# A linear-attention and MoE kernel: one queue for batch 0, a new order for its first stages, joined loads and stores

## The chip, the core and the metric

The kernel runs on one core of a Trainium2 chip. The metric is device time in microseconds (us) of one execution; where several executions are given, their median. The core has five instruction streams: PE (TensorE, matmuls; PEld is its weight loads), DVE (VectorE), ACT (ScalarE), POOL (GpSimd) and SP (SyncE, which here only issues DMAs). DMAs are issued from SP and from POOL, and run on 16 DMA engines. POOL's DMAs convert float32 to bfloat16 on their way.

## The reference

```
q, k, v: (8, 8, 576, 64) float32          # batch, heads, sequence, head_dim
w_in: (512, 2048), w_out: (2048, 512), beta: (2048,)

phi(x) = where(x > 0, x, exp(x) - 1) + 1
kv  = einsum('bhsd,bhse->bhde', phi(k), v)
z   = sum(phi(k), over s)
x   = einsum('bhsd,bhde->bhse', phi(q), kv) / (einsum('bhsd,bhd->bhs', phi(q), z) + 1e-6)
x   = x with heads side by side: (4608 tokens, 512)
h   = x @ w_in
out = (h * sigmoid(beta * h)) @ w_out      # (4608, 512) float32
```

## The kernel before

**Tiling.** The sequence of a batch is cut as 576 = 64 groups (g) x 9 (j). A load puts 64 groups of four heads on one half of the 128 partitions and those of the other four heads on the other half, so that each partition row is 9 x 64 numbers in one piece. The tokens of one j are 64 rows. Tokens of two j make a token tile of 128 (t = 0 to 3); the ninth j makes a tile of 64 (t = 4). Four tiles of a batch (512 tokens) are one block of the two large products; the 64 left over of all eight batches make a ninth block of 512 (`xT_tail`).

**A batch's attention.** `phi_part` (exp on ACT), `phi_relu` and `phi_min` (DVE) make phi(k) and phi(q). `kv_both` sums phi(k)'s products with v over the groups, with a column of ones for the denominators; a mask keeps the blocks that belong to one head. phi(q) is transposed, by `q_trans` on PE (a PSUM tile, then a copy) or by `q_trans_dma` (two DMA transposes on SP). `numer` makes numerators and denominators of one token tile, divides, and leaves it in `xs`; it has one PSUM buffer. `xs` is transposed into `xT` by `x_trans` (PE and a copy) or by `x_trans_dma` (SP).

**A block's products.** The H phase (`h_phase`) has 16 steps `ff` of four matmuls 128x512; each ends in a `silu` on ACT, which writes `g`. The Y phase (`y_phase`) has four token tiles of 16 matmuls; `y_out` copies each from PSUM to one of three `y_sb` buffers on DVE and stores it with two DMAs of 64 rows from SP (L309 to L312). H, Y and warm-up matmuls share four PSUM buffers (`mmps`); all transposes and `kv_both` share two (`miscps`).

**Order.** It is written out by hand: each engine runs its instructions in the order of the text. `at(side, n, ...)` places the next batches' attention between the steps of the phases. In the steady loop (from L495) batch b+1's `kv_both`, `numer` and x transposes stand in block b's H phase, batch b+2's phi, q transposes and loads in its Y phase. Batches 3 to 7 use DMA transposes for q and x, batches 0 to 2 PE transposes.

**The start (L90 to L124, L341 to L442).** Batch 0's k and q come half by POOL's casting DMAs, half by SP in float32 into `stage`; its v by POOL. `w_in` follows on POOL in four loads, then batch 1's k and q. `w_out` comes by SP in float32, the first part held back until the third `w_in` load has landed (`add_manual_dep`); half of it lies in `g_sb[1]`, which block 1's silu will overwrite, half in `stage`. It is scaled by 1/beta on its way to bfloat16: `w_out_scale`, parts 0 and 1 on DVE, 2 and 3 on POOL. `idle` issues warm-up matmuls on data that nobody needs. Block 0's first four H steps run in two column halves, beside batch 0's last token tiles. Block 0's Y phase goes over the parts i of `w_out`: 0, 1 and 2 for all four tiles, then batch 1's q transposes, kv and numerators with part 3 between them, then all four `y_out`.

The store's rows, which the change touches (L304):

```
    def rows(b, j):
        return out[b * S : (b + 1) * S, :].rearrange("(g j) m -> j g m", j=J)[j]
```

Of the kernel before, what the change touches and what calls it, by code (L numbers as in the profile page):

```python
# [16 lines left out]
def kernel(  # L17
# [51 lines left out]
    k0f = stage[:, 0:1152].rearrange("p (h j d) -> p h j d", h=2, j=J)  # L69
    q0f = stage[:, 1152:2304].rearrange("p (h j d) -> p h j d", h=2, j=J)  # L70
    v0b = vf[0].rearrange("p h j d -> p (h j d)").bitcast(BF16)[:, 0:2304].rearrange(
        "p (h j d) -> p h j d", h=4, j=J
    )

    def heads(src, b, hh, h0, n):
        return src[b, hh * 4 + h0 : hh * 4 + h0 + n].rearrange(
            "h (g j) d -> g h (j d)", j=J
        )

    def load(eng, dst, src, b, h0=0, n=4):  # L80
        return [
            eng.dma_start(  # L82
                out=dst[hh * G : (hh + 1) * G].rearrange("p h j d -> p h (j d)"),
                in_=heads(src, b, hh, h0, n),
            )
            for hh in range(2)
        ]


    nc.vector.memset(warm, 0.5)  # L90
    load(nc.gpsimd, xk[0][:, 0:2], k, 0, 0, 2)
    load(nc.sync, k0f, k, 0, 2, 2)
    load(nc.gpsimd, xq[0][:, 0:2], q, 0, 0, 2)
    load(nc.sync, q0f, q, 0, 2, 2)
    beta_row = consts.tile([FC, P], F32)
    nc.sync.dma_start(out=beta_row, in_=moe_beta.rearrange("(c p) -> c p", p=P))
    load(nc.gpsimd, v0b[:, 0:2], v, 0, 0, 2)
    load(nc.gpsimd, v0b[:, 2:4], v, 0, 2, 2)
# [12 lines left out]
    load(nc.gpsimd, xq[1], q, 1)  # L111

    def load_w_out(i, after=None):
        d = nc.sync.dma_start(out=w_out_f[i], in_=w_out_v[:, i * 4 : (i + 1) * 4, :])
        if after is not None:
            tc.add_manual_dep(d.ins, after.ins.name, SYNC, reason="share of the queues")
# [4 lines left out]
    nc.vector.memset(kvmask[D:P, :, 1, :], 1.0)  # L121
    for i in range(2):
        nc.vector.memset(vaug[i][:, :, :, :, D : D + 2], 1.0)

    def idle(n, cols=512):
        for _ in range(n):
            wp = mmps.tile([P, 512], F32, tag="mm", name="warm_ps")
            nc.tensor.matmul(wp[:, 0:cols], warm[:, 0:P], warm[:, 0:cols], start=True, stop=True)
# [4 lines left out]
    def phi_part(b, a, pr, x):  # L133

        e = work.tile([P, 2, J, D], BF16, tag="e", name="e", bufs=3)
        nc.scalar.activation(e, x, ACTF.Exp)  # L136
        st[b, a, pr, "e"] = e
# [9 lines left out]
    def phi_min(b, a, pr):  # L147
        nc.vector.tensor_tensor(  # L148
            st[b, a][:, pr].rearrange("p j (h d) -> p j h d", h=2),
            st[b, a, pr, "e"].rearrange("p h j d -> p j h d"),  # L150
            st[b, a, pr, "r"].rearrange("p h j d -> p j h d"),
            ALU.min,
        )

    def xin(b, a, pr):
        if b == 0:
            if pr == 1:
                return k0f if a == "k" else q0f
            return (xk if a == "k" else xq)[0][:, 0:2]
        return (xk if a == "k" else xq)[b % NX][:, 2 * pr : 2 * pr + 2]  # L160

    def v_copy(eng, b, pr):
        src = v0b if b == 0 else vf[b % 2]
        eng.tensor_copy(  # L164
            vaug[b % 2][:, pr, :, :, 0:D],
            src[:, 2 * pr : 2 * pr + 2].rearrange("p h j d -> p j h d"),
        )
# [46 lines left out]
    def q_trans_dma(b):  # L214
        st[b, "qTd"] = work.tile([P, 2, 2 * J, G], BF16, tag="qT", name="qTd")
        for hh in range(2):
            nc.sync.dma_start_transpose(
                out=st[b, "qTd"][:, hh],
                in_=st[b, "q"][hh * G : (hh + 1) * G].rearrange("p a j c -> p (a j c)"),
            )  # L220

    def q_stat(b, t, hh, pr, n):
        if (b, "qTd") in st:
            return st[b, "qTd"][:, hh, pr * J + 2 * t : pr * J + 2 * t + n // G, :].rearrange(
                "p j g -> p (j g)"
            )
        return st[b, "qT"][:, t, pr, hh, 0:n]

    def numer(b, t):
        n = P if t < NT - 1 else G  # L230
        nps = numps.tile([P, 2, 512], F32, tag="num", name="nps")
        for hh in range(2):
            for pr in range(2):
                nc.tensor.matmul(  # L234
                    nps[:n, hh, pr * 2 * EA : (pr + 1) * 2 * EA],
                    q_stat(b, t, hh, pr, n), st[b, "kv"][:, hh, pr, :],
                    start=True, stop=True, skip_group_check=True,
                )
# [5 lines left out]
        xs = work.tile([P, 2, 4, D], BF16, tag="xs", name="xs", bufs=4)  # L244
        nc.vector.tensor_mul(  # L245
            xs[:n], nv[:, :, :, 0:D], rden[:n, :, :, None].to_broadcast([n, 2, 4, D])
# [8 lines left out]
    def x_trans(b, t, eng):  # L255
        n = P if t < NT - 1 else G
        xv = st[b, "xs", t].rearrange("p a h d -> p (a h d)")
# [11 lines left out]
    def x_trans_dma(b, t):  # L269
# [3 lines left out]
            in_=st[b, "xs", t][:n].rearrange("p a h d -> p (a h d)"),  # L273
# [30 lines left out]
    def rows(b, j):  # L304
        return out[b * S : (b + 1) * S, :].rearrange("(g j) m -> j g m", j=J)[j]

    def y_out(b, t, yp, c0=0, c1=512, eng=None):
        y_sb = work.tile([P, DM], F32, tag="y_sb", name="y_sb", bufs=3)
        (eng or nc.vector).tensor_copy(y_sb[:, c0:c1], yp[:, c0:c1])  # L309
        for i in range(2):  # L310
            dst = rows(b, 2 * t + i) if b < B else rows(2 * t + i, J - 1)
            nc.sync.dma_start(out=dst[:, c0:c1], in_=y_sb[i * G : (i + 1) * G, c0:c1])  # L312

    def w_out_scale(eng, i):
        for c in range(4):
            ff = 4 * i + c
            eng.tensor_scalar(  # L317
                w_out_sb[i][:, c, :], w_out_f[i][:, c, :], rbeta[:, ff : ff + 1],
                None, ALU.mult,
            )  # L320
# [18 lines left out]


    idle(10)  # L341
    bps = miscps.tile([P, FC], F32, tag="misc", name="bps")
    nc.tensor.matmul(bps, beta_row, ident16, is_transpose=True, start=True, stop=True)
# [3 lines left out]
    beta_s = consts.tile([P, FC], F32)  # L347
    nc.vector.tensor_copy(beta_s, bps)
# [4 lines left out]

    phi_all(0, "k")
    idle(6)
    phi_all(0, "q")
    for t in range(2):
        q_trans(0, t, nc.vector)
    kvp0 = {}
    for pr in range(2):  # L360
        v_copy(nc.vector, 0, pr)
    kv_tile(0)
    idle(4)
    for pr in range(2):
        for hh in range(2):
            kvp0[hh, pr] = mm_tile("kvp0")[:, 0 : 2 * EA]
        kv_products(0, (pr,), kvp0)
        for hh in range(2):
            nc.vector.tensor_mul(
                st[0, "kv"][:, hh, pr, :], kvp0[hh, pr],  # L370
                kvmask.rearrange("p a g e -> p a (g e)")[:, 0, :],
            )
    for t in range(2, NT):
        q_trans(0, t, nc.scalar)
    numer(0, 0)
    numer(0, 1)
    x_trans(0, 0, nc.scalar)
    numer(0, 2)
    x_trans(0, 1, nc.scalar)
    hps = {}  # L380
    for ff in range(4):
        hps[ff] = mm_tile("h_ps")
        h_mm(0, xT[0], ff, hps[ff], 0, 256)
        if ff == 0:
            numer(0, 3)
        if ff == 1:
            x_trans(0, 2, nc.scalar)
        if ff == 2:
            numer(0, 4)
            x_trans(0, 3, nc.scalar)  # L390
        if ff == 3:
            x_trans(0, 4, nc.scalar)
    for ff in range(4):
        h_mm(0, xT[0], ff, hps[ff], 256, 512)
        silu(0, ff, hps[ff])
    load_w_out(0, w_in_dma[2])
    load_w_out(1)
    load_w_out(2)
    load_v(1)
    load_w_out(3)  # L400
# [4 lines left out]
    load_kq(2)  # L405
    w_out_scale(nc.vector, 0)
    w_out_scale(nc.vector, 1)


    yps = [mm_tile("y_ps") for _ in range(4)]  # L410
    phi_all(1, "k")
    phi_all(1, "q")
    for i in range(3):
        if i == 2:
            w_out_scale(nc.gpsimd, 2)
        for t in range(4):
            y_mm(0, t, i, yps[t])
    for pr in range(2):
        v_copy(nc.gpsimd, 1, pr)
    w_out_scale(nc.gpsimd, 3)  # L420
    load_v(2)
    for t in range(3):
        q_trans(1, t, nc.scalar)
    kv_both(1)
    for t in range(3, NT):
        q_trans(1, t, nc.scalar)
    numer(1, 0)
    y_mm(0, 0, 3, yps[0])
    numer(1, 1)
    x_trans(1, 0, nc.scalar)  # L430
    y_mm(0, 1, 3, yps[1])
    numer(1, 2)
    x_trans(1, 1, nc.scalar)
    y_mm(0, 2, 3, yps[2])
    numer(1, 3)
    x_trans(1, 2, nc.scalar)
    y_mm(0, 3, 3, yps[3])
    numer(1, 4)
    x_trans(1, 3, nc.scalar)
    for t in range(4):  # L440
        y_out(0, t, yps[t])
    x_trans(1, 4, nc.scalar)  # L442
# [32 lines left out]
    sh = {}  # L475
    at(sh, 2, lambda: load_kq(3))
    at(sh, 6, lambda: [v_copy(nc.gpsimd, 2, pr) for pr in range(2)], lambda: load_v(3))
    h_phase(1, xT[1], sh)
    sy = {}
    phi_all(2, "k")  # L480
    at(sy, 0, lambda: phi_all(2, "q"))
    at(sy, 5, lambda: kv_both(2))
    at(sy, 7, lambda: q_trans(2, 0, nc.vector))
    at(sy, 8, lambda: q_trans(2, 1, nc.vector), lambda: numer(2, 0))
    at(sy, 9, lambda: q_trans(2, 2, nc.vector), lambda: numer(2, 1))
    at(sy, 10, lambda: x_trans(2, 0, nc.vector), lambda: q_trans(2, 3, nc.vector))
    at(sy, 11, lambda: numer(2, 2), lambda: phi_all(3, "q"))
    at(sy, 12, lambda: x_trans(2, 1, nc.vector), lambda: q_trans(2, 4, nc.vector))
    at(sy, 13, lambda: numer(2, 3), lambda: x_trans(2, 2, nc.vector))
    at(sy, 14, lambda: numer(2, 4), lambda: phi_all(3, "k"))  # L490
    at(sy, 15, lambda: x_trans(2, 3, nc.vector), lambda: x_trans(2, 4, nc.vector))
# [3 lines left out]
    for b in range(2, B + 1):  # L495
# [4 lines left out]
        if n < B:  # L500
            if n == 3:
                at(sh, 1, lambda: [v_copy(nc.gpsimd, 3, pr) for pr in range(2)], lambda: load_v(4))
            at(sh, 3, lambda: kv_both(n))
# [41 lines left out]
```

## Time and profile before

| what | us |
|---|---|
| median of three runs | 327.95 |
| lowest and highest of them | 327.88, 329.81 |
| the profiled execution | 329.76 |
| its span, first to last instruction | 328.0 |
| PE busy in the span | 295.7 |
| DVE, ACT, POOL busy | 119.4, 160.2, 55.6 |
| first H matmul of block 0 | 28.73 |
| first full-width H matmuls, in a row | 37.26 |
| first Y matmul of block 0 | 47.35 |
| first H matmul of block 2 | 114.61 |
| a later block (146.7 to 177.0) | 30.3 |

The mean granted PE clock is 0.951 of full speed. DMAs move 40.82 MB in 47510 packets.

How to read it: `L279` is line 279 of the kernel. In the slices, the span is cut into 40 equal parts (8.2 us each) and a digit is a busy share in tenths; `PEclk` is the granted clock in tenths. `out<-in` names the tiles. The chain is the work that ended last, followed back from the last instruction; `issue` in it is time for which the profile shows no wait. The DMA share of a stretch is the mean busy share of the 16 engines; it can exceed 1, since packets overlap. "To landing" is from an issue to the DMA's last semaphore update.

### The profile page before, as it was taken

Reading aid. Unit: us, or ns where it says so; the run is one execution under the profiler, and the core shown is the slowest. Engines: PE = TensorE matmul, PEld = TensorE weight load, DVE = VectorE, ACT = ScalarE, POOL = GpSimd, SP = SyncE. Lnnn points to the kernel's source line nnn. Section 1 sums busy time; section 2 is a strip of 40 time slices with the busy share of each in tenths; the row PEclk is TensorE's granted clock in tenths of the full one; section 3 lists DMA queues with packets and bytes.
Section 4 is the critical chain, followed back from the end, with each engine's and each line's share of the span. In section 5 each row is a group of like instructions: output and inputs, shape, how many; then the busy total and the mean of one; then the engine's idle time right before and its main releaser. Section 6 shows DMA issues by size and latency. Waiting matters only on the chain.

```text
span 328.0 us, 4511 instructions
## 1 busy us (share of the span) xinstructions
PE 295.7 (90%) x1739; PEld 144.9 (44%) x1767; DVE 119.4 (36%) x272; ACT 160.2 (49%) x208; POOL 55.6 (17%) x70
## 2 busy tenths in 40 slices
PE   5377899786999499999999999999999999999994
PEld 1145544532455244445444544554454444444443
DVE  1564606351048905532551436154425110010011
ACT  0612885362692247816682585378256018306600
POOL 8520067940220004102300200020000000000000
PEclk9565999997899979999999999999999999999999
DMA  7999998299519187987988525942723140041032
GB/s 171 210 207 280 286 273 208 37 187 211 132 26 189 27 155 143 174 146 196 129 132 191 141 43 82 199 113 28 152 50 64 40 88 10 0 97 33 0 66 65
DMA packets 47510, 40.82 MB, mean 124 GB/s; under 512 B 26352, under 2 KB 36864, under 8 KB 47488
## 3 DMA queue, kind: packets, MB, share of 16 engines
q1 hardware_dynamic: 36608, 28.99, 40.3%
q0 software_dynamic: 10880, 11.54, 22.5%
q8 instruction: 14, 0.23, 0.3%
q14 instruction: 8, 0.07, 0.1%
HBM read 36.71 MB, written 9.44 MB: 141 GB/s over the span
## 4 chain that ended last, share of the span: by engine, by line
PE 82%; DVE 7%; DMA 4%; issue 3%; ACT 2%; SPq 1%; DVEq 0%
PE h_ps L279 38%; PE y_ps L297 36%; PE nps L234 4%; PE kvp L174 3%; DMA beta_row<-in_moe_beta_dram 2%; DVE xs L245 2%; DMA out_dram<-y_sb 2%; DVE y_sb L309 1%; PE qtp L202 1%; SPq L82 1%; DVE rden L243 1%; ACT qT L210 1%; DVE r L141 1%; DVE phi_q L148 1%; PE xtp L260 1%
## 5 line engine op out<-in xcount | busy, mean ns | idle before, releaser
L287 ACT ACTIVATE g<-h_ps,beta_c 128x512 bf16<-128x512 f32 x144 | 98.2, 687 | 105.5 <-PE h_ps L279 103.3
L279 PE MATMUL h_ps<-xT,w_in 128*128 128x512 bf16 (+1 forms) x513 | 122.8, 386 | 8.5 <-DVE y_sb L309 3.5
L297 PE MATMUL y_ps<-w_out,g 128*128 128x512 bf16 (+2 forms) x580 | 127.2, 374 | 1.3 <-DVE y_sb L309 0.6
L279 PEld LDWEIGHTS <-w_in 128*128 128x128 bf16 x592 | 57.5, 100 | 71.7 <-issue 13.9
L297 PEld LDWEIGHTS <-g 128*128 128x128 bf16 x592 | 57.0, 98 | 64.9 <-issue 0.8
L309 DVE COPY y_sb<-y_ps 128x512 f32<-128x512 f32 (+2 forms) x37 | 24.8, 673 | 88.0 <-PE y_ps L297 82.2
L164 POOL CAST vaug<-vf 128x1152 bf16<-128x1152 f32 x14 | 16.6, 1214 | 123.2 <-DMA vf<-in_v_dram 98.1
L245 DVE TENSOR_TENSOR xs<-nps,rden 128x512 bf16<-128x512 f32 (+1 forms) x40 | 27.6, 690 | 1.4
L148 DVE TENSOR_TENSOR phi_k<-e,r 128x1152 bf16<-128x1152 bf16 x16 | 12.1, 787 | 25.6 <-ACT e L136 25.6
L136 ACT ACTIVATE e<-xk 128x1152 bf16<-128x1152 bf16 x15 | 16.7, 1151 | 7.5 <-DVE phi_q L148 7.4
L242 DVE TENSOR_SCALAR den<-nps 128x8 f32<-128x8 f32 (+1 forms) x40 | 6.5, 164 | 32.0 <-PE nps L234 32.0
L148 DVE TENSOR_TENSOR phi_q<-e,r 128x1152 bf16<-128x1152 bf16 x16 | 11.8, 753 | 13.9 <-ACT e L136 13.9
L136 ACT ACTIVATE e<-xq 128x1152 bf16<-128x1152 bf16 x15 | 16.5, 1151 | 0.0
L317 POOL TENSOR_SCALAR w_out<-stage,rbeta 128x512 bf16<-128x512 f32 x8 | 12.6, 1591 | 20.8 <-DMA stage<-in_moe_w_out_dram 20.8
L190 DVE TENSOR_TENSOR kv_bd<-kvp,kvmask 128x260 bf16<-128x260 f32 x14 | 5.3, 423 | 26.9 <-PE kvp L174 26.9
L279 PE MATMUL h_ps<-xT_tail,w_in 128*128 128x512 bf16 x63 | 13.9, 379 | 0.1
L136 ACT ACT_TABLE_LOAD x7 | 9.0, 1283 | 8.9 <-DMA xk<-in_k_dram 8.8
L82 POOL DMA_DIRECT2D xk<-in_k_dram x16 | 10.2, 645 | 9.7 <-ACT e L136 5.3
L174 PE MATMUL kvp<-vaug,phi_k 64*128 64x130 bf16 x288 | 10.9, 229 | 0.4 <-ACT qT L210 0.3
L82 POOL DMA_DIRECT2D xq<-in_q_dram x16 | 10.4, 663 | 4.5 <-DMA w_in<-in_moe_w_in_dram 3.8
L174 PEld LDWEIGHTS <-phi_k 64*128 64x128 bf16 x288 | 9.3, 100 | 4.1 <-issue 2.6
L234 PEld LDWEIGHTS <-qTd 128*128 128x128 bf16 (+1 forms) x100 | 7.5, 100 | 6.8 <-DVE xs L245 2.1
(46 smaller groups left out, 116.1 us busy)
## 6 DMA issues: line engine op xcount, KB each, us to landing
out_dram<-y_sb SPq DMA_DIRECT2D x70, 128.0 KB, 2.4
vf<-in_v_dram SPq DMA_DIRECT2D x14, 576.0 KB, 7.3
xk<-in_k_dram POOLq DMA_DIRECT2D x14, 288.0 KB, 6.6
xq<-in_q_dram POOLq DMA_DIRECT2D x14, 288.0 KB, 9.6
w_in<-in_moe_w_in_dram POOLq DMA_DIRECT2D x4, 512.0 KB, 10.6
g<-in_moe_w_out_dram SPq DMA_DIRECT2D x2, 1024.0 KB, 13.1
stage<-in_moe_w_out_dram SPq DMA_DIRECT2D x2, 1024.0 KB, 22.5
stage<-in_k_dram SPq DMA_DIRECT2D x2, 288.0 KB, 4.3
```

What stands on the lines that cost most here:

```text
L82: eng.dma_start(out=dst[hh * G : (hh + 1) * G].rearrange("p h j d -> p h (j d)"), in_=heads(src, b, hh, h0, n),)
L136: nc.scalar.activation(e, x, ACTF.Exp)
L148: nc.vector.tensor_tensor(st[b, a][:, pr].rearrange("p j (h d) -> p j h d", h=2), st[b, a, pr, "e"].rearrange("p h j d -> p j h d"), st[b, ...
L164: eng.tensor_copy(vaug[b % 2][:, pr, :, :, 0:D], src[:, 2 * pr : 2 * pr + 2].rearrange("p h j d -> p j h d"),)
L174: nc.tensor.matmul(ps[hh, pr], st[b, "k"][r, pr, j, :], vaug[b % 2][r, pr, j, :, 0:EA], start=(j == 0), stop=(j == J - 1), skip_group_chec ...
L234: nc.tensor.matmul(nps[:n, hh, pr * 2 * EA : (pr + 1) * 2 * EA], q_stat(b, t, hh, pr, n), st[b, "kv"][:, hh, pr, :], start=True, stop=True ...
L245: nc.vector.tensor_mul(xs[:n], nv[:, :, :, 0:D], rden[:n, :, :, None].to_broadcast([n, 2, 4, D]))
L279: nc.tensor.matmul(hp[:, c0:c1], w_in_sb[ff // 4][:, kc, (ff % 4) * P : (ff % 4 + 1) * P], x[:, kc, c0:c1], start=(kc == 0), stop=(kc == K ...
L287: nc.scalar.activation(g_sb[b % 2][:, ff, :], hp, ACTF.Silu, scale=beta_c[:, ff : ff + 1])
L297: nc.tensor.matmul(yp[:, c0:c1], g_sb[b % 2][:, ff, t * P : (t + 1) * P], w_out_sb[i][:, c, c0:c1], start=(ff == 0), stop=(ff == FC - 1), ...
L309: (eng or nc.vector).tensor_copy(y_sb[:, c0:c1], yp[:, c0:c1])
L317: eng.tensor_scalar(w_out_sb[i][:, c, :], w_out_f[i][:, c, :], rbeta[:, ff : ff + 1], None, ALU.mult,)
```

## The change

1. **Loads.** `load` is one DMA of 128 partitions where it was two of 64. Heads 2i and 2i+1 now lie on the two halves of the partitions, so `xs` is laid out `[4, 2, 64]` and its writes are strided. Batch 0's k, q and v come by POOL alone, in six calls of two head pairs each; SP issues only beta there. Batch 1's v comes cast by POOL behind its k and q. `w_out`'s four loads are issued early on SP, part 0 held for the third `w_in` load, part 2 for batch 1's q; batch 2's q on POOL is held for part 2 of `w_out`.
2. **Stores.** `y_out` issues one DMA of 128 partitions for two j. In the built program the DRAM side of the store has the counts 2x64x512 (64x512 before) and the SBUF side 128 partitions of 512. In the ninth block it is 128x512, 128x320 and 128x192.
3. **Batch 0.** ACT's Exp and Silu tables are asked for ahead by two one-column activations (`tiny`). phi(k)'s column sums (`row_products` with `ones`), then all denominators and reciprocals (`dens`, `recips`) come ahead of the products with v; v is used as it landed, without `v_copy`. The numerators have both halves of the PSUM buffer in turn (`numer0`). phi(q)'s second pair is done in two pieces. The five qT copies are all on ACT. Block 0's first four H steps run by token tiles of 128 columns (`h0_tile`), with their silus behind the last tile.
4. **Block 0's Y phase.** Parts 0 and 1 of `w_out`, then batch 1's q transposes and kv, then parts 2 and 3 in turns with its numerators; `w_out_scale` of parts 2 and 3 is shared by ACT and DVE; each `y_out` follows its tile. Half of batch 1's v copy is on DVE. phi(q) of batch 2 follows.
5. **Batch 2.** q is transposed by DMA in block 1's H phase, x by DMA in its Y phase; `kv_both(2)` is at step 4, the numerators at 6 to 10.
6. **Later.** `kv_both` is one step later (4). The last token tile's numerators read 128 columns of `qTd`, which has two columns more and a small memset on POOL.

```diff
+    vb = [
+        a.rearrange("p h j d -> p (h j d)").bitcast(BF16)[:, 0 : 4 * J * D].rearrange(
+            "p (h j d) -> p h j d", h=4, j=J
+        )
+        for a in vf
+    ]
     def load(eng, dst, src, b, h0=0, n=4):
...
+        rows = src[b].rearrange("h (g j) d -> (h g) (j d)", j=J)
+        return eng.dma_start(
+            out=dst[:, h0 : h0 + n].rearrange("p h j d -> p h (j d)"),
+            in_=rows.rearrange("(i p) e -> p i e", p=P)[:, h0 : h0 + n],
+        )
+
+    def hold(d, after):
+        tc.add_manual_dep(d.ins, after.ins.name, SYNC, reason="share of the queues")
...
+    tiny = consts.tile([P, 2], BF16)
+    nc.scalar.activation(tiny[:, 0:1], warm[:, 0:1], ACTF.Exp)
+    for h0 in (0, 2):
+        load(nc.gpsimd, xk[0], k, 0, h0, 2)
+    for h0 in (0, 2):
+        load(nc.gpsimd, xq[0], q, 0, h0, 2)
+    for h0 in (0, 2):
+        load(nc.gpsimd, vb[0], v, 0, h0, 2)
...
     load(nc.gpsimd, xk[1], k, 1)
-    load(nc.gpsimd, xq[1], q, 1)
+    q1_dma = load(nc.gpsimd, xq[1], q, 1)
+    load(nc.gpsimd, vb[1], v, 1)
...
+    load_w_out(0, w_in_dma[2])
+    load_w_out(1)
+    w_out2_dma = load_w_out(2, q1_dma)
+    load_w_out(3)
...
     def q_trans_dma(b):
-        st[b, "qTd"] = work.tile([P, 2, 2 * J, G], BF16, tag="qT", name="qTd")
+        st[b, "qTd"] = work.tile([P, 38, G], BF16, tag="qT", name="qTd")
+        nc.gpsimd.memset(st[b, "qTd"][:, 36:37], 0.0)
...
+    def norm(b, t, n, num, rd):
+        xs = work.tile([P, 4, 2, D], BF16, tag="xs", name="xs", bufs=4)
         nc.vector.tensor_mul(
-            xs[:n], nv[:, :, :, 0:D], rden[:n, :, :, None].to_broadcast([n, 2, 4, D])
+            xs[:n].rearrange("p i a d -> p a i d"), num,
+            rd[:, :, :, None].to_broadcast([n, 2, 4, D]),
         )
...
     def rows(b, j):
-        return out[b * S : (b + 1) * S, :].rearrange("(g j) m -> j g m", j=J)[j]
+        return out[b * S : (b + 1) * S, :].rearrange("(g j) m -> j g m", j=J)[j : j + 2]
 
     def y_out(b, t, yp, c0=0, c1=512, eng=None):
...
-        for i in range(2):
-            dst = rows(b, 2 * t + i) if b < B else rows(2 * t + i, J - 1)
-            nc.sync.dma_start(out=dst[:, c0:c1], in_=y_sb[i * G : (i + 1) * G, c0:c1])
...
+        if b < B:
+            dst = rows(b, 2 * t)
+        else:
+            dst = out.rearrange("(b g j) m -> j b g m", b=B, j=J)[J - 1, 2 * t : 2 * t + 2]
+        nc.sync.dma_start(
+            out=dst[:, :, c0:c1],
+            in_=y_sb[:, c0:c1],
+        )
...
+    def row_products(pr, mov, col, n):
+        for j in range(J):
+            for hh in range(2):
+                r = slice(hh * G, (hh + 1) * G)
+                nc.tensor.matmul(
+                    kvz[hh][:, col : col + n],
+                    st[0, "k"][r, pr, j, :],
+                    mov(r, j),
+                    start=(j == 0), stop=(j == J - 1), skip_group_check=True,
+                )
...
+    for pr in range(2):
+        row_products(pr, lambda r, j: ones[r], 256 + 2 * pr, 2)
...
+    nc.scalar.activation(tiny[:, 1:2], warm[:, 0:1], ACTF.Silu)
     for t in range(2):
-        q_trans(0, t, nc.vector)
...
+        q_trans(0, t, nc.scalar)
+    for t in range(2, NT):
+        q_trans(0, t, nc.scalar)
+    dens((0, 1))
+    recips(0, 2, P)
+    dens((2, 3, 4))
+    recips(2, 4, P)
+    recips(4, 5, G)
...
+        row_products(pr, lambda r, j: vb[0][r, 2 * pr : 2 * pr + 2, j, :], pr * P, P)
...
+    def h0_tile(t):
+        for ff in range(4):
+            h_mm(0, xT[0], ff, hps[ff], t * P, (t + 1) * P)
...
+    for i in range(2):
         for t in range(4):
             y_mm(0, t, i, yps[t])
-    for pr in range(2):
-        v_copy(nc.gpsimd, 1, pr)
-    w_out_scale(nc.gpsimd, 3)
-    load_v(2)
-    for t in range(3):
+    for t in range(NT):
         q_trans(1, t, nc.scalar)
+    v_copy(nc.gpsimd, 1, 0)
+    v_copy(nc.vector, 1, 1)
+    hold(load(nc.gpsimd, xq[2], q, 2), w_out2_dma)
+    load(nc.gpsimd, xk[2], k, 2)
     kv_both(1)
...
+    w_out_scale(2, 2)
     numer(1, 0)
-    y_mm(0, 0, 3, yps[0])
+    y_mm(0, 0, 2, yps[0])
...
+    y_mm(0, 0, 3, yps[0])
+    y_out(0, 0, yps[0])
+    x_trans(1, 4, nc.scalar)
+    for t in range(1, 4):
+        y_mm(0, t, 3, yps[t])
         y_out(0, t, yps[t])
...
+    at(sh, 0, lambda: q_trans_dma(2))
+    at(sh, 4, lambda: load_kq(3))
+    at(sh, 8, lambda: [v_copy(nc.gpsimd, 2, pr) for pr in range(2)], lambda: load_v(3))
     h_phase(1, xT[1], sh)
...
+    at(sy, 4, lambda: kv_both(2))
+    at(sy, 5, lambda: phi_all(3, "q"))
+    for t in range(NT):
+        at(sy, 6 + t, lambda t=t: numer(2, t))
+        at(sy, 7 + t, lambda t=t: x_trans_dma(2, t))
+    at(sy, 10, lambda: phi_all(3, "k"))
     y_phase(1, sy)
...
-            at(sh, 3, lambda: kv_both(n))
+            at(sh, 4, lambda: kv_both(n))
```

## The prediction, written before the changed kernel ran

> **What bounds the kernel now.** I read the page's slices and chain first, then the busy time by stage, then the chain piece by piece where a stage is longer than its matmuls.
>
> ```profile
> PE   5377899786999499999999999999999999999994
> ...
> PEclk9565999997899979999999999999999999999999
> ...
> PE 82%; DVE 7%; DMA 4%; issue 3%; ACT 2%; SPq 1%; DVEq 0%
> ```
>
> TensorE is the chain. From the middle of the run PE reads 9 in every slice; the holes and the low clock lie in the first 15 slices (123 us). The stages (columns: stretch, then busy us of PE, PEld, DVE, ACT, POOL, then clock, DMA share, GB/s):
>
> ```profile
> 0.00:28.70 28.70, 15.08 (x95) 7.55 (x96) 13.36 (x36) 8.24 (x10) 13.86 (x28) 0.72 1.08 207
> ...
> 47.30:69.90 22.60, 19.51 (x153) 10.19 (x152) 11.17 (x24) 11.13 (x15) 19.61 (x18) 1.00 0.73 150
> 69.90:90.80 20.90, 17.22 (x67) 7.19 (x70) 3.19 (x6) 11.85 (x17) 2.23 (x2) 0.84 0.81 167
> 90.80:115.60 24.80, 19.78 (x158) 10.79 (x160) 19.11 (x45) 11.90 (x11) 2.60 (x4) 0.98 0.44 82
> ...
> 146.70:177.00 30.30, 30.14 (x183) 14.59 (x184) 12.95 (x29) 17.88 (x22) 4.63 (x6) 1.00 0.91 154
> ...
> 237.60:267.90 30.30, 30.14 (x182) 14.56 (x184) 8.81 (x21) 11.00 (x16) 0.00 (x0) 1.00 0.29 60
> 267.90:295.50 27.60, 27.44 (x126) 12.53 (x128) 2.77 (x4) 10.99 (x16) 0.00 (x0) 1.00 0.18 39
> ```
>
> A settled batch takes 30.3 us and PE is full. Its 64 H and 64 Y matmuls of 128x512 are 13.84 us per phase (64 x 0.216, the pace of the 47 in 10.1 us that end H0). The stretches before 115.6 are where time can be won. In them the chain shows one plain wait, in order of time:
>
> ```profile
> 69.87 0.61 DVE y_sb L309
> 70.49 0.54 SPq L312
> 71.08 6.31 DMA out_dram<-y_sb
> ...
> 77.51 0.70 DVE y_sb L309
> ...
> 78.25 11.89 PE h_ps L279 x41
> ```
>
> Batch 0's fourth output copy needs the first's buffer, whose store lands late among loads; PE stands still for 3.24 us, and the clock drops to 0.5. Last, the DMAs (queue, count, KB, us to landing) and two short stretches for rates:
>
> ```profile
> out_dram<-y_sb SPq DMA_DIRECT2D x70, 128.0 KB, 2.4
> ...
> qTd<-phi_q SPq DMA_TRANSPOSE x10, 4.8
> ```
>
> ```profile
> 20.00:24.00 4.00, 3.55 (x52) 2.75 (x50) 1.59 (x5) 0.98 (x3) 0.61 (x1) 0.66 1.24 206
> ...
> 48.00:50.00 2.00, 1.95 (x10) 0.88 (x10) 0.00 (x0) 1.97 (x3) 2.00 (x2) 1.00 1.05 338
> ```
>
> At 20 to 24 only w_in arrives, cast from f32: 206 GB/s landed is 412 fetched, 25.8 per DMA engine (16 engines). At 48 to 50 only f32 arrives: 338, or 21.1 per engine.
>
> **The start.** Six casting calls of 288 KB land at 206 GB/s, one per 1.4 us. The first is issued at about 1.2 and lands 4 us later (the quietest xk call: 3.8), so 5.3, then 6.8, 8.2, 9.6, 11.0, 12.5 for v. Exp (1.15) no longer waits for a 1.28 us table load at 8.8. phi(k)'s sums, the beta chain (five DVE steps of 0.2, moved ahead of phi(q)) and phi(q) make phi(q) whole at about 12.8. The five qT copies go all to ACT (0.59 each) behind the early Silu load, whose 1.28 us end before phi(q) is there: done 15.6. Denominators 0.8, v products 2 x 1.03 at half clock (36 took 2.06), masks 0.5: first numer about 20.2, first H0 matmul 22.9, against 28.73. H0 by token tiles is 64 matmuls of 128 columns for 32 of 256: at half clock 16 x 0.107 = 1.7 us a tile, four tiles 6.9 against 8 x 0.85 = 6.8, so nothing. The full-width part starts about 29 instead of 37.3, with silu's table already in. Gain 8; as low as 4 if PE stays at half clock, as high as 10.
>
> **Batch 0's Y phase with batch 1.** The same 18 transposes, 36 products and five numer chains (1.64 each, DVE's 1.1 in them) run beside 32 Y matmuls instead of 16. The scales of w_out 2 and 3 leave POOL (8 x 1.59) for ACT and DVE (0.6 and 0.42 each); those on DVE stand ahead of numer, 1.7 in all. I count 23.4 from end of H0 to end of Y0, against 23.1 (47.35 to 70.5): Y0 ends at 62.6. The two loads that hold() delays, and POOL's queue behind them (batch 3's loads, a small memset), have 15 us to spare. The outputs now come 0.86 us apart, after those loads. If a store lands in 2.4, the 3.24 us wait goes and so does the low clock after it (43 matmuls in 12.54 for 9.3, so 3.2): gain 6.4 - 0.3.
>
> **Batch 1's Y phase with batch 2.** 18 q and 18 x transposes on PE with ten DVE copies (0.42) become DMAs. PE keeps 13.84 + 1.16 + 5 x 0.25; DVE, in order, holds 2 us more: about 19.5 against 23.8, plus 0.8 of issue and 0.9 of low clock at 115: gain 6. Behind it come up to 0.3 x 5 for the 64-wide numer weights (0.35 and a hole beside 0.23) and 0.6 for the last second store issue: gain 2. The strided write of xs I cost at nothing: twice its 0.69 would still fit the 1.96 us from numer to numer.
>
> Sum so far: 8 + 6 + 6 + 2 = 22, a span of 306.
>
> **The stores decide.** Two stores of 64 rows become one whose DRAM side has counts 2x64x512. Every DMA of before has an outermost count of 16, 64 or 128. No row shows how a count of 2 is dealt to the engines. One end: over 16, as before. The 267.9:295.5 row is almost only stores: 0.18 x 27.6 = 5.0 us of each engine per batch, 1.2 us for each of four new stores. Other end: one engine per outer index, two engines, 64 packets of 2 KB each where a store had 8 per engine. Then a store takes 64 x 80 ns = 5.1 us (25.8 GB/s) to 64 x 97 = 6.2 (21.1); by the share row it would be 8 x 5.0 = 40 us per batch, but that counts overlapping packets (shares reach 1.24). I take the second end, because 16, 64 and 128 all divide over 16 engines and this one breaks it, and 5.4 us a store, since only two engines draw on the memory.
>
> The Trainium skill's page "DMA: Bandwidth & Descriptors", section "Why a DMA increments its semaphore by 16 and not by 1", says that a copy uses the largest number of engines up to 16 that divides the outermost counts of both sides; here that is two. Its "Rules for kernel authors" also advise one 128-partition transfer over two halves, which speaks for the edit and would give 306; the first rule gives the sum below. With that page's 27 GiB/s per engine a store is estimated at 4.5 us. No run here shows either yet.
>
> Work of those two engines per batch: stores 21.6; v 32 packets, 3; k and q 64 packets, 6; x transposes 3.8 (0.29 x 30.3 of the 237.6:267.9 row less 5.0); q's, as many packets, 3.8. That is 38 against PE's 30.3, and SP's queue is in order on each engine: v and the transposes stand behind the stores. Step by step:
> - Y0's first store is issued at 60.6. The smallest stores land in 1.9, so this one lands at 60.6 + 1.9 + 5.4 = 67.9. DVE's fourth copy waits for it, with phi(q) of batch 2 behind it; PE stands from 65.2 to 69.6. With 1.7 of half clock H1 ends at 82.6 instead of 76.4.
> - The queue: four stores to 84, v(2) to 87, q's transposes to 91, so kv(2) waits 3 us for v. Then v(3) 3, batch 1's first two stores 10.8, k and q of batch 4 between 6, x's four transposes 3.1, landing 1.9: H2 can start at 116, against 114.6 now. What the start won is gone here.
> - The other two stores (10.8) and q's transposes of batch 3 (3.8) follow: numer(3), due at 122, waits to 131. H2 ends at 131 + 11 x 0.865 + 1.2 + 1.7 of low clock = 143.4, Y2 at 157.2, against 146.7 now: +10.5.
> - The next two batches go at the queue's 38 and not at 30.3, the one after, with no more loads, at about 30: +15, less 1 for slack.
>
> So 10.5 + 14 - 2 (the numer holes and the last issue) = +22.5: a span of 350.5. The profiled execution took 329.8 with a span of 328.0, so it would take 352; the median of the runs, 327.95, lies 1.8 below it, level with the span. I forecast 351.
>
> **Rivals.**
>
> - Stores over 16 engines: all gains stay, 306 (302 to 313 by the start's bounds and DVE in Y1). For it: 2.4 us to landing in every row. Against: no row has such a pattern. This ends faster. It decides as long as a store keeps below 3.4 us of an engine: four of them and the 16.6 of other work then fit in 30.3. Chance 0.15.
> - Two engines at a contended price, 97 ns (the 48 to 50 row) to 125 (5.0 us over 32 packets, over the overlap of 1.24): 24.8 to 32 us of stores and 41 to 49 in all per batch, 3 to 10 more than my 38 in some five batches: 366 to 400. For it: v's f32 rows at 243 GB/s in 82 to 86, 15 per engine. Against: there all 16 compete. Chance 0.17.
> - Two engines, but the queues' slack hides more (80 ns, transposes at their fastest, no low clock): per batch 33 to 35 and no stall before H2: 15 less or more, 320 to 335. Chance 0.10.
> - My case, 335 to 368: 0.58.
>
> Leaving out the even spread and the far end, 318 to 395 holds about 8 in 10. A per cent, 3.3 us, is about what a measurement can tell from no change: faster 0.16, the same 0.04, slower 0.80.
>
> **What would show it.** First H0 matmul at 23, Y0's end near 63, and the start is right. out_dram landing at 7 us or more at batch 0, DVE y_sb waiting for out_dram in Y0, and PE waiting for xT and qTd in H2 show the stores. If they land in 2.5, the forecast is wrong and 306 comes. If they take 7 but batches 3 to 5 still run at 30.3, the per-batch sum is wrong.

## The result, and the profile after

The changed kernel takes 369.36 us (median of 4 runs, 368.49 to 372.91), the kernel before 327.91 (4 runs, 326.55 to 329.81). The ratio is 1.128, with a 95% interval of 1.118 to 1.138. The profiled execution took 372.9 with a span of 371.1, against 329.8 and 328.0 before, so the spans differ by 43.1. Here and below, an interval leaves out executions that took over 1.5% longer than the fastest of the same kernel; of e1_split's four only one is then left, so it has no interval.

From the page of the changed kernel: the busy slices, the granted clock, the DMA share, what the DMAs moved, the chain, and the row of the stores.

```profile
span 371.1 us, 4514 instructions
...
PE   5789988598860175998997579989996999999995
...
PEclk9558999989895585999999669999998999999999
DMA  7999990149993997394499539741931931101102
GB/s 109 205 222 284 279 207 15 41 145 125 255 51 42 144 65 201 47 197 159 67 52 139 125 145 64 114 158 61 84 86 51 64 62 51 51 14 51 53 34 79
...
PE 40%; DMA 30%; issue 15%; SPq 7%; DVE 3%; POOL 2%; ACT 1%; DVEq 0%; POOLq 0%; ACTq 0%
...
out_dram<-y_sb SPq DMA_DIRECT2D x35, 256.0 KB
```

PE's share of the chain fell from 82% to 40%; DMA, issue and SP's queue have 52%. Slices 13 to 15 (111 to 139 us) read 0, 1, 7 for PE, and holes now come in the middle of the run too, where the kernel before reads 9 throughout. The late slices give the cause away: 51 GB/s again and again, at a DMA share of 1 tenth. The last slice is the tail, whose joined store is one run of 128 rows; it moves 79. The last row has no landing time, where the kernel before's has 2.4: the trace has two closing 4-byte packets for such a store, where it has 16 for a DMA with a landing time.

Two stretches of the changed kernel (columns as in the tables above: stretch, busy us of PE, PEld, DVE, ACT, POOL, clock, DMA share, GB/s):

```profile
66.00:73.00 7.00, 3.16 (x15) 1.33 (x14) 0.88 (x2) 3.68 (x5) 0.00 (x0) 1.00 0.13 43
110.00:118.00 8.00, 0.00 (x0) 0.00 (x0) 0.00 (x0) 0.00 (x0) 0.00 (x0) 0.60 0.14 35
```

In the first only batch 0's stores run: 0.13 of 16 engines is two. From 72 to 77 us the packet records have 25 packets of 2 KB per us, 84 ns each, and the stores end at 72.03, 77.16, 82.28 and 87.4: one per 5.13 us. In the second nothing computes at all, and two engines work: in every 2 us some 22 packets of a k or q load (1152 B, 107 ns) and some 22 of a store (2 KB, 96 ns). The other fourteen engines have finished their part of the loads. These two, by the even counts, take a packet from one queue and one from the other, so beside a load a store's packet comes round every 182 ns on an engine (88 packets on two engines in these 8 us) instead of every 80.

What waited, in the changed kernel (waiter, what it waited for: total us, times, longest):

```profile
DVE xs L258 <- DMA xT<-xs: 39.1, 5, 19.8
DVE y_sb L323 <- DMA out_dram<-y_sb: 37.8, 5, 12.6
...
PE h_ps L293 <- DMA xT<-xs: 23.6, 2, 19.4
...
PE h_ps L293 <- DVE y_sb L323: 14.2, 5, 4.7
...
PE nps L244 <- DMA qTd<-phi_q: 6.5, 2, 5.9
```

The worst stretch in the chain, ahead of batch 2's H phase (start, us, what):

```profile
100.27 9.14 SPq L285
...
109.51 5.61 SPq L285
...
115.22 2.20 SPq L285
...
117.51 10.61 DMA xT<-xs
128.12 0.09 issue
128.21 1.01 PE h_ps L293 x2
```

L285 is the DMA transpose of x. The first of the four takes SP 9.14 us to issue, the second 5.61, and the fourth lands 10.61 after its issue began. PE stood from 108.76 to 128.21.

### The profile page after: what moved, and what is told of

It is laid out like the page before. It is cut to its first block, busy times and chain, and to the rows that moved or that the text cites. A ratio compares the mean times of both kernels' runs of the same rounds, so it can differ in the third digit from the quotient of the medians.

```text
span 371.1 us, 4514 instructions
## 1 busy us (share of the span) xinstructions
PE 306.4 (83%) x1787; PEld 149.7 (40%) x1816; DVE 115.0 (31%) x263; ACT 164.4 (44%) x217; POOL 36.4 (10%) x52
## 3 DMA queue, kind: packets, MB, share of 16 engines
q0 software_dynamic: 11664, 12.72, 25.5%
## 4 chain that ended last, share of the span: by engine, by line
PE 40%; DMA 30%; issue 15%; SPq 7%; DVE 3%; POOL 2%; ACT 1%; DVEq 0%; POOLq 0%; ACTq 0%
PE h_ps L293 21%; PE y_ps L311 16%; DMA out_dram<-y_sb 9%; DMA xT<-xs 9%; DMA xq<-in_q_dram 8%; SPq L285 5%; SPq L227 2%; PE kvp L183 2%; DMA stage<-in_moe_w_out_dram 2%; DVE y_sb L323 2%; PE nps L244 1%; DMA qTd<-phi_q 1%; POOL xk L80 1%; DMA xT_tail<-xs 1%; ACT e L150 1%
## 5 line engine op out<-in xcount | busy, mean ns | idle before, releaser
L293 PE MATMUL h_ps<-xT,w_in 128*128 128x512 bf16 (+1 forms) x547 | 130.0, 391 | 38.4 <-DMA xT<-xs 23.6
L293 PEld LDWEIGHTS <-w_in 128*128 128x128 bf16 x624 | 61.0, 104 | 106.9 <-issue 30.0
L173 POOL CAST vaug<-vf 128x1152 bf16<-128x1152 f32 x12 | 13.8, 1175 | 173.7 <-DMA vf<-in_v_dram 173.7
L244 PE MATMUL nps<-kv_bd,qTd 128*128 128x130 bf16 x120 | 12.9, 230 | 8.1 <-DMA qTd<-phi_q 6.5
L150 ACT ACTIVATE e<-xq 128x1152 bf16<-128x1152 bf16 (+2 forms) x17 | 17.9, 1098 | 0.9 <-DMA xq<-in_q_dram 0.5
L161 DVE TENSOR_TENSOR phi_k<-e,r 128x1152 bf16<-128x1152 bf16 x16 | 11.6, 751 | 19.0 <-ACT e L150 19.0
L244 PEld LDWEIGHTS <-qTd 128*128 128x128 bf16 x120 | 9.4, 102 | 17.1 <-DMA qTd<-phi_q 7.3
L161 DVE TENSOR_TENSOR phi_q<-e,r 128x1152 bf16<-128x1152 bf16 (+2 forms) x17 | 11.7, 717 | 3.7 <-ACT e L150 3.5
L279 ACT COPY xT<-xtp 128x512 bf16<-128x512 bf16 x8 | 4.7, 584 | 17.8 <-PE xtp L274 17.8
L139 PE MATMUL warm_ps<-warm 128*128 128x512 bf16 x17 | 8.2, 630 | 2.0 <-DVE warm L91 1.5
L154 DVE TENSOR_SCALAR r<-xk 128x1152 bf16<-128x1152 bf16 x16 | 6.8, 462 | 3.6 <-DMA xk<-in_k_dram 3.6
## 6 DMA issues: line engine op xcount, KB each, us to landing
xk<-in_k_dram POOLq DMA_DIRECT2D x7, 576.0 KB, 10.8
```

Source lines behind the costliest of these rows:

```text
L139: nc.tensor.matmul(warm_ps[:, 0:cols], warm[:, 0:P], warm[:, 0:cols], start=True, stop=True)
L150: nc.scalar.activation(st[b, a, pr, "e"][:, :, j0:j1], x[:, :, j0:j1], ACTF.Exp)
L161: nc.vector.tensor_tensor(st[b, a][:, pr, j0:j1].rearrange("p j (h d) -> p j h d", h=2), st[b, a, pr, "e"][:, :, j0:j1].rearrange("p h j d ...
L173: eng.tensor_copy(vaug[b % 2][:, pr, :, :, 0:D], src[:, 2 * pr : 2 * pr + 2].rearrange("p h j d -> p j h d"),)
L244: nc.tensor.matmul(nps[: qs.shape[-1], hh, pr * 2 * EA : (pr + 1) * 2 * EA], qs, st[b, "kv"][:, hh, pr, :], start=True, stop=True, skip_gr ...
L293: nc.tensor.matmul(hp[:, c0:c1], w_in_sb[ff // 4][:, kc, (ff % 4) * P : (ff % 4 + 1) * P], x[:, kc, c0:c1], start=(kc == 0), stop=(kc == K ...
```

## The experiments

My theory going in: a store of 2x64x512 goes over two DMA engines, and what else those engines and SP's queue have to carry waits behind it; the other parts of the change are gains, smaller than forecast. First rival: some other part costs much of the 41 us. Second rival: the joined store is slow for another reason (its pattern, or being joined). H1 and Y1 stand for block 1's H and Y phase, and so on. Times are medians, with the ratio to the kernel before and its 95% interval; the kernel before took 327.3 to 327.9 beside them.

| kernel | us | ratio |
|---|---|---|
| changed kernel | 369.36 | 1.118 to 1.138 |
| e1_split | 319.68 (314.74 to 321.71) | none formed |
| e2_before_joined | 376.69 | 1.140 to 1.156 |
| e3_four | 324.18 | 0.979 to 0.993 |
| e3_eight | 318.08 | 0.963 to 0.974 |
| e4_ysb8 | 365.08 | 1.103 to 1.116 |
| e5_pool | 348.16 | 1.041 to 1.055 |
| e6_pe | 317.58 | 0.961 to 0.969 |
| e7_hold | 326.84 | 0.992 to 1.000 |
| e8_order | 319.81 | 0.957 to 0.970 |
| e9_start | 318.62 | 0.967 to 0.978 |
| e10_both | 317.65 | 0.958 to 0.969 |

**e1_split: the changed kernel, with the store alone undone.**

```
-            dst = rows(b, 2 * t)
...
-            out=dst[:, :, c0:c1],
-            in_=y_sb[:, c0:c1],
...
+        for i in range(2):
+            dst = rows(b, 2 * t + i) if b < B else rows(2 * t + i, J - 1)
+            nc.sync.dma_start(out=dst[:, c0:c1], in_=y_sb[i * G : (i + 1) * G, c0:c1])
```

> The changed kernel with one thing undone: each output store is again two stores of 64 rows. Theory (the joined store goes over two DMA engines only): the stores land in 2 to 3 us again, the waits of PE on xT, qTd and y_sb (about 45 us in the changed kernel's trace) go, and the gains of the other parts are left. The trace of the changed kernel shows a start gain of 4.3 where I had 8, so 306 + 4 = 310; 304 to 318. Rival (other parts of the edit, such as batch 2's transposes by DMA or the loads' new order, cost a good part of the 41 us): 335 or more.

Measured 319.68: 50 us gone with one edit, a little above the theory's 318 and far from the rival's 335. All four runs lie below the seven of the kernel before beside them (325.97 to 329.48). Its page has the stores as in the kernel before:

```profile
out_dram<-y_sb SPq DMA_DIRECT2D x70, 128.0 KB, 2.4
```

The first rival is out: the rest of the change, taken together, is a gain of some 8, not a cost. But it isn't the 22 that I had summed.

**e2_before_joined: the kernel before, with the joined store alone.** The diff is that of the change in `rows` and `y_out`, and nothing else.

> The kernel before with one thing of the change: two stores of 64 rows become one of 2x64x512. Theory (two engines): each store takes 5.1 us on two engines as in the changed kernel; work per settled batch on these two about 38 us against PE's 30.3, and the transposes stand behind the stores: slower by 25 to 60, so 353 to 388. Rival (the store alone is harmless, another part or the sum of them does it): 325 to 335.

Measured 376.69, so +49, the same price as in the changed kernel (369.36 - 319.68 = 50): the store is sufficient by itself. The waits of this kernel:

```profile
DVE y_sb L309 <- DMA out_dram<-y_sb: 42.3, 5, 11.2
PE h_ps L279 <- DVE y_sb L309: 34.6, 8, 9.4
...
PE nps L234 <- DMA qTd<-phi_q: 9.3, 2, 8.7
```

Where batch 2 is transposed on PE, H2 doesn't wait for xT, and PE pays on the output buffers instead: 34.6 against 14.2.

**e3_four and e3_eight: as many joined stores of as many bytes, with another outermost count.** The output's rows come out in another order, so these two serve the question alone. The diff is e3_four's; in e3_eight n is 8.

```
-            dst = rows(b, 2 * t)
+            n = 4
+            w = 2 * G // n
+            q, r = divmod(t, G // w)
+            dst = out[b * S : (b + 1) * S, :].rearrange("(g j) m -> j g m", j=J)[
+                n * q : n * q + n, r * w : r * w + w
+            ]
```

> The changed kernel with as many stores of as many bytes, but the DRAM side of each as 4x32x512 in place of 2x64x512 (the rows of batches' first eight parts come out in another order, so the output is permuted; the work is the same). Theory (engines used = outermost count): four engines, 32 packets of 2 KB on each at 84 ns, 2.7 us a store. That is 10.8 us of stores a batch on an engine in place of 21, 27 in all, below PE's 30.3: 306 to 322. Rival (any store that isn't one run of rows is slow, or the joining itself): as the changed kernel, 360 to 375. Second rival (the cost falls in proportion, so half of it stays): 335 to 345.

> The same with 8x16x512 on the DRAM side (output rows permuted too). Theory: eight engines, 16 packets on each, 1.35 us a store; as with the split stores within 3 us, so 304 to 318. Rival (pattern or joining): 360 to 375.

Measured 324.18 and 318.08. Batch 0's stores alone, in e3_four and then in e3_eight:

```profile
67.00:72.00 5.00, 2.63 (x13) 1.08 (x11) 0.94 (x2) 2.97 (x4) 0.00 (x0) 1.00 0.24 84
```

```profile
67.00:70.00 3.00, 2.87 (x14) 1.18 (x12) 0.78 (x3) 2.79 (x5) 0.00 (x0) 1.00 0.49 162
```

Two, four and eight engines show as 0.13, 0.24 and 0.49 of 16, at 43, 84 and 162 GB/s; a packet still takes 84 ns in the median. So the outermost count of the DRAM side sets the number of engines, and the second rival is out: these stores are joined, and their rows are as far apart. The time doesn't fall in proportion, which was e3_four's second rival, though at 324.18 it is 2 above the theory's range. Halving the work per engine takes away 45 of the 50 us, as it should if four engines' share fits under PE's 30 us a batch (27 by the expectation's sum). The rest sits where the loads are densest: PE waits 2.4 us for y_sb in H1 and 5.3 for q's transpose in H2, and has neither wait in e1_split.

**e4_ysb8: the changed kernel with eight output buffers.**

```
-        y_sb = work.tile([P, DM], F32, tag="y_sb", name="y_sb", bufs=3)
+        i = st["n"] = (st.get("n", -1) + 1) % 8
+        y_sb = stage[:, i * DM : (i + 1) * DM]
```

> The changed kernel, with the joined stores, but with eight output buffers in place of three (slices of the stage tile, free by then). Theory (two engines have more work per batch than PE, and the transposes stand behind the stores): PE's waits on y_sb, 14 of its 45 us of gaps, go, but more stores then stand ahead of the transposes and the waits on xT and qT grow: 355 to 370. Rival (three buffers were too few for a slower store, and nothing else): the gaps on y_sb and those that follow from them go, 335 or less.

Measured 365.08: 4 less, in the theory's range. The waits of PE in e4_ysb8:

```profile
PE h_ps L293 <- DMA xT<-xs: 25.4, 2, 19.2
...
PE kvp L183 <- POOL vaug L173: 7.4, 1, 7.4
...
PE nps L244 <- DMA qTd<-phi_q: 6.5, 2, 5.9
PE h_ps L293 <- DVE stage L324: 4.1, 3, 1.6
```

The wait on output buffers fell from 14.2 to 4.1. The waits on xT and qT, which the theory had growing, are 25.4 for 23.6 and 6.5 as before. What came up instead is 7.4 on v: its copy starts as late as in the changed kernel (90.50, there 90.89), behind the same four stores, and PE now gets to it sooner. So more buffers only move the wait, and the theory's time came by a wait that it hadn't named.

**e5_pool: the changed kernel, joined stores issued by POOL's queue.**

```
-        nc.sync.dma_start(
+        nc.gpsimd.dma_start(
```

> The changed kernel with the joined stores issued by POOL's queue instead of SP's; transposes and v stay on SP's. It parts two halves of my theory. If the 38 us of work a batch on the two engines is what counts: 355 to 375, as now. If it is the order in SP's queue (a transpose behind up to three stores of 5.13 us): the transposes no longer stand behind the stores, and with the gaps on xT and qT (about 30 us) gone it is 325 to 345. That the stores spread over 16 engines there: 315 to 322, landing in under 3 us.

Measured 348.16: two of the four runs, at 351.4 and 351.7, lie between the two halves' ranges, and two, at 344.5 and 344.9, at the upper end of the second. POOL's queue cuts the same store differently, as two rows of e5_pool's DMA view show:

```profile
q0 software_dynamic: 28896, 22.27, 35.4%
...
out_dram<-y_sb POOLq DMA_DIRECT2D x35, 256.0 KB, 10.3
```

That is 17232 packets more than POOL's queue has in the changed kernel (11664), and a store lands in 10.3 us. Nor do these stores share the same two engines. Late in the run, where only stores are moved, e5_pool has

```profile
306.50:308.50 2.00, 2.00 (x11) 0.88 (x9) 0.69 (x1) 0.00 (x0) 0.53 (x1) 1.00 0.32 83
```

and 83 GB/s is more than the 51 that two engines move in the changed kernel. So consecutive stores overlap here, on more engines than two. This run changes both halves of the theory at once and parts nothing. What it does show: with the stores off SP's queue and so spread, batches 3 to 5 take 31.5 each (H phases begin at 157.23, 188.72, 220.24, 251.70), where the changed kernel takes 35.8, 39.9 and 31.5. Which of the two did it, this run doesn't say.

**e6_pe: e1_split, with batch 2's q and x transposed on PE.** The lines of Y1's side work are those of the kernel before, and the DMA transposes of batch 2 go:

```
-    at(sh, 0, lambda: q_trans_dma(2))
...
-        at(sy, 7 + t, lambda t=t: x_trans_dma(2, t))
+    at(sy, 10, lambda: x_trans(2, 0, nc.vector), lambda: q_trans(2, 3, nc.vector))
...
```

> The changed kernel with split stores (e1_split), and with batch 2's q and x transposed on PE with DVE copies, as in the kernel before. In e1_split Y1's start to H2's start took 25.9 (24.0 in the kernel before), where I had forecast a gain of 6. Theory (the fourth x transpose lands 8.5 us after its issue, among batch 4's loads, so the DMA form has no gain here): 316 to 322, within 2 of e1_split. Rival (the DMA form does save some 6 us, and e1_split lost them elsewhere): 324 to 328.

Measured 317.58, 2.1 below e1_split and in the theory's range: the DMA form of batch 2's transposes doesn't bring the 6 that I had. From Y1's start to H2's start it takes 23.9 on PE (e6_pe) and 23.2 to 25.9 by DMA (e3_eight, e9_start, e1_split).

**e7_hold: e1_split, with batch 4's k and q loads held.**

```
-            at(sh, 0, lambda: q_trans_dma(3), lambda: load_kq(4))
+            at(sh, 0, lambda: q_trans_dma(3), lambda: [
+                hold(load(nc.gpsimd, x[4 % NX], src, 4), st[2, "xd", 3])
+                for x, src in ((xk, k), (xq, q))
+            ])
```

> e1_split with batch 4's k and q loads held until batch 2's fourth x transpose has landed. Theory (these loads are what makes that transpose land in 8.5 us instead of 2.4 to 4): H2 starts 4 us earlier and the low clock after the gap goes: 312 to 316. Rival (something else delays it, such as the stores or q's transposes, or the held loads are late for batch 4): as e1_split, 317 to 321.

Measured 326.84, slower than e1_split, where the theory said faster and the rival the same. Its mechanism is there all the same: the fourth x transpose lands 2.4 us after its issue (8.5 in e1_split), and H2 starts 19.4 after Y1, which is the 19.5 of my forecast. But the held loads now run beside q's transposes of batch 3, in e7_hold's chain:

```profile
104.10 1.39 SPq L227
...
105.53 12.88 DMA qTd<-phi_q
```

The transpose lands 12.9 us after its issue, and PE stands 11.45 in H2. I had priced where the load left, and not where it went.

**e8_order, e9_start, e10_both: two attempts at a faster version.** e8_order also issues batch 3's q transposes right behind the x transposes and holds the loads until these land. e9_start takes two things out of the start's chain. e10_both does both.

```
-    at(sy, 10, lambda: phi_all(3, "k"))
+    at(sy, 10, lambda: phi_all(3, "k"), lambda: q_trans_dma(3))
...
-            at(sh, 0, lambda: q_trans_dma(3), lambda: load_kq(4))
+            at(sh, 0, lambda: [hold(load(nc.gpsimd, x[4 % NX], src, 4), st[3, "qd"])
+                               for x, src in ((xk, k), (xq, q))])
```

```
-    nc.scalar.activation(tiny[:, 1:2], warm[:, 0:1], ACTF.Silu)
     for t in range(2):
         q_trans(0, t, nc.scalar)
     for t in range(2, NT):
         q_trans(0, t, nc.scalar)
+    nc.scalar.activation(tiny[:, 1:2], warm[:, 0:1], ACTF.Silu)
...
-        idle(2)
     numer0(0)
```

> The changed kernel with split stores (e1_split), with batch 3's q transposes issued right behind batch 2's fourth x transpose, and batch 4's k and q loads held until those have landed. Theory (what a load of 576 KB does to a transpose issued beside it is the cost: 8.5 us to landing for the fourth x transpose in e1_split, 13 for q's in e7_hold): Y1's start to H2's start 19.4 as in e7_hold plus up to 2 for two more transposes, and no wait of PE on qTd in H2: 306 to 313. Rival (the delay moves on again, to v, k or q of batch 4 or to the next transposes): 316 to 327.

> e1_split with two changes in the start: Silu's table load goes behind the five qT copies, and the two pairs of idle matmuls between the v products and the first numer go. In the trace of e1_split both stand in the chain: 1.28 us of table load between the last exp and the first qT copy, and 0.97 twice. Theory (these are the part of my 8 us start gain that did not come): the first numer at 18.8 to 20.5 instead of 21.7, Y0 2 to 3 us earlier: 314 to 317.5. Rival (without the idle matmuls the clock stays at 0.5 for longer and takes it back): 318 to 322.

> The two together: the orders of e8_order and the start of e9_start. If both theories hold, 303 to 311, faster than both kernels; if the start gives nothing, as e8_order.

Measured 319.81, 318.62 and 317.65: the first two lie in their rivals' ranges, and the third is as e8_order. In e8_order H2 starts 19.4 after Y1 again, and q's transposes no longer wait, but v's copy now stands behind the held loads in POOL's queue, in e8_order's chain:

```profile
102.24 0.49 POOL xk L80
...
103.71 1.19 POOL vaug L173
104.90 0.04 issue
104.94 2.25 PE kvp L183 x36
```

PE waits 2.9 us for it, and 4.4 for an output buffer after Y2. This execution, 322.0, is the longest of six (from 314.15), so what the shorter ones wait for isn't shown. What e7_hold and this profile have in common is that the delay moves along with the loads. In e9_start the first numer comes at 19.1 (21.7 in e1_split) and Y0 at 40.5, as forecast. But e6_pe and e8_order, with the start untouched, have Y0 at 40.7 and 40.8 in their profiles, and e1_split at 43.6, so this difference isn't shown to be the edit's (the clock goes with it, as the next section shows); 1 us in the median isn't either. e3_eight, e6_pe, e8_order, e9_start and e10_both take 3 to 4% less than the kernel before, and their intervals overlap, so none of them is shown to be the best.

## Why the prediction was right, and where its terms were off

I forecast 351, inside a range of 318 to 395, and slower; it took 369. The step that decides is right: two engines, from the outermost count of 2. A store takes 5.13 us where I put 5.4. The Trainium skill's page "DMA: Bandwidth & Descriptors" gives this count in "Why a DMA increments its semaphore by 16 and not by 1", and runs with 2, 4 and 8 agree with it. The 4.5 us a store that I estimated from that page's rate is below the 5.13 measured, and the measurement decides. Its advice under "Rules for kernel authors", one transfer of 128 partitions instead of two halves, taken without that count, costs 50 us here: the two halves had 64 outermost each, and the joined store has 2.

By its time alone the result is 1 us outside my own case (335 to 368) and inside the rival of two engines at a contended price (366 to 400). By its mechanism it isn't that rival: a store's packet takes 84 ns alone and 96 beside a load, where the rival needs 97 to 125, and batches 3 and 4 take 35.8 and 39.9, where it has 41 or more. The time is over for the reasons below, and the wide range covers them.

The walk, against the profiled span (20.6 over my 350.5):

| step, as forecast | forecast | measured | over |
|---|---|---|---|
| Y0's end | 62.6 | 66.4 | +3.8 |
| Y0's end to H1's end, with PE's wait for y_sb (4.4; it was 4.1) | 20.0 | 19.8 | -0.2 |
| H1's end to H2's start | 33.4 | 42.0 | +8.6 |
| H2 with numer(3)'s wait, to Y2's start | 27.4 | 27.8 | +0.4 |
| the rest, from Y2's end, over the kernel before's 181.4 | +12 | +19.9 | +7.9 |

- **The start** was forecast 8 shorter, to the end of H0. In this profile it is 4.3, and over nine profiles with this start Y0 begins at 39.6 to 43.6, against 47.2 and 45.9 in the two with the old one. Three things in the trace aren't in my sum: the early Silu load isn't over before phi(q), as I had it, but stands behind the last exp in ACT's order (12.42 to 13.71) ahead of the first qT copy; the second xk call lands at 7.98, not 6.8, and each later call with it; and two pairs of idle matmuls at half clock stand between the v products and the first numer, which I left out. The spread goes with the granted clock. The changed kernel and e5_pool, which have the same start, from 21 to 33 us:

```profile
21.00:33.00 12.00, 10.35 (x107) 8.97 (x107) 4.04 (x7) 3.89 (x8) 0.00 (x0) 0.64 1.17 252
```

```profile
21.00:33.00 12.00, 10.14 (x118) 7.42 (x118) 3.34 (x5) 6.97 (x13) 0.00 (x0) 1.00 1.17 255
```

Y0 begins at 42.9 and at 39.6. Five of the nine read 0.60 to 0.66 there and have Y0 at 42.5 to 43.6; four read 0.86 to 1.00 and have it at 39.6 to 41.3. At a like clock the gain is the same 4 to 5: 47.2 against 42.5 to 42.9 (0.64 to 0.66) and 45.9 against 41.3 (0.86). So the gain came out at half my 8 at either clock, and the condition that I gave for 4, a PE that stays at half clock, isn't the reason. e9_start and e10_both, at 0.77 and 0.76, have Y0 at 40.5 and 40.9, somewhat below the 41.3 at 0.86, so a part of that may be the edit's. No run sets the clock by itself.
- **H2's start** is the step that failed by most. I had one pair of k and q loads between the stores, 6 us. Two pairs are issued ahead of it, batch 4's at 93.5 and batch 5's at 105.1, 32 packets of 107 ns each per load on an engine: 4 x 32 x 0.107 = 13.7. The 7.7 more is close to the miss of 8.6, but no run isolates it, so this cause is argued and not shown. I also had SP issue a transpose in no time; it stands up to 9.14 on one, so the four went out one after another.
- **Batches 3 and 4** at 38 each: measured 35.8 and 39.9, and 75.7 for 76 is right as a sum, but no run shows that it is the engines' 38 us of work that makes it so. **Batches 5 and 6**, at 30 and a settled 30.3 by my count since the loads run out, took 31.5 and 34.7. Their four stores are 20.5 us of two engines but must be handed over within a Y phase of 13.8, with three buffers: PE waits for y_sb (1.2 and 2.95). Together they are 5.9 over my count, and the sum per batch doesn't see it, since it has no buffers in it. The gains that I set against it came to less.

The gains without the store, by e3_eight's profile (span 316.4, 11.6 under before): the start 3.6 for 8, the y_sb wait with its low clock 5.7 for 6.1, Y1 0.8 for 6, the rest 1.5 for 2. **Y1** fails as a reason, not only in size. I costed what PE and DVE no longer do, and my sum for Y1 has no term for the transposes' landing. Beside batch 4's loads the last of them lands 8.5 us after its issue in e1_split and 6.7 in e9_start, in whose chain it stands:

```profile
94.54 6.74 DMA xT<-xs
101.28 0.04 issue
101.32 0.80 PE h_ps L293 x2
```

So PE's work was taken off a path that DMA then closed: e7_hold shows the 19.5 when the loads are away, and what it costs to put them elsewhere. "Stores over 16 engines: 306" would have been wrong as well; e1_split is that case, at 319.7.

What stays open: what holds SP while it issues a transpose. One of q's, issued at 79.69, is held for 7.98 us and let go at 87.67, just after the fourth store's end at 87.4, so a full queue on the two engines fits; but one is held for 5.86 in e1_split and one for 7.38 in e8_order, where no store goes over two engines, and no run takes this apart. Nor did any run settle how the loss divides between the two engines' work and the order in SP's queue.

## What to carry to other kernels

Before joining two DMAs into one, write down the outermost count of both sides after the program has merged what it can: a 2 in front of 64 rows meant two engines here. Then add up the work of the busiest engine per period, not of the mean, and walk what is queued behind it in order, with buffers and issue included. When a transfer takes over work of a compute engine, price its landing in the stretch where it will run, beside the loads that are due there; and when a load is moved out of the way, price it where it goes.

## What the runs showed of the hardware that I had not expected

- Two engines that serve a load and a store take packets in turn (22 and 22 in 2 us, 107 and 96 ns). The last part of a load that is spread over 16 engines is so held up on two of them, while fourteen are idle: in the median a k load took 10.8 us to land, against 7.0 in e3_eight.
- A DMA transpose held SP's queue for 9.14 us at its issue in the changed kernel, where 1.2 to 1.3 is usual.
- The same 2x64x512 store lands 10.3 us after its issue from POOL's queue; SP's first of batch 0, with no store ahead of it, ended 7.7 after its issue (64.34 to 72.03). But POOL's stores overlapped, at up to 83 GB/s in a stretch of 2 us, where SP's went one after another, 5.13 us each, at 51.
